# Packing the half-full last chunks of two batches in an MLP, and reordering the first loads

## Chip, cores, metric

One core of a Trainium2 chip. The time is device microseconds for one launch; a run of all kernels here is called fast when it is within 1.5% of the fastest of its kernel, and all runs quoted were. A difference is given as a ratio: the mean time of one kernel's fast runs over the mean of the other's from the same rounds, so not quite the ratio of the medians quoted beside it. Its 95% interval is some 0.1 to 0.15% to each side, about 0.5 us; a difference between two such differences is uncertain by some 0.7 us.

In the profiles PE is TensorE's matrix multiplications and PEld its weight loads, DVE is VectorE, ACT is ScalarE, POOL is GpSimd, SP is SyncE; L356 is line 356 of that kernel. A matmul is written with the shape of its stationary operand (`128*64`: 128 rows, 64 columns; the one that PEld loads) and then that of its moving operand (`128x512`: 512 moving columns). An eviction is the instruction on ACT or DVE that copies a result out of PSUM. A head pair is two heads that are worked on together, and qsrow a table, made from an iota (the numbers 0, 1, 2, ...), by which q is multiplied. `[2.76 <-PE ps_y L356]` says that the engine stood idle for 2.76 us before the line and what ended that.

## The reference, cut to what matters

```python
# batch 8, heads 8, sequence 576, head_dim 64: d_model 512; MLP width 2048
scores = scale * q @ k.T                       # per head
ret    = scores * where(i >= j, gamma**(i-j), 0)
x      = (ret @ v)  -> [batch, 576, 512]
u      = x + (x.T @ U @ V).T                   # low-rank mixer over tokens, rank 32
out    = u + relu(u @ w_ch1) @ w_ch2           # the MLP, 512 -> 2048 -> 512
```

576 tokens are four chunks of 128 and one of 64. That last 64 is what the change is about.

## The kernel before

It is written for a scheduler that fixes each engine's order of instructions and inserts the semaphores; `nc.any` lets it choose ACT or DVE. Per batch: attention (retention in chunks, head pairs one after another through one PSUM buffer `po`), the mixer, the two MLP products.

```python
def make_consts():                       # after batch 0's q, k, v loads are issued
    nc.gpsimd.iota(iota_col, pattern=[[1, SP]], ...)
    ... qsrow = exp(iota_col * log(gamma))       # ACT; q is multiplied by it
    ... U_sb, V_sb loads

def mlp_tail(b, u_t, uT_t):
    y1_t = y1_pool.tile([P, NF, S], BF16, ...)           # y1_pool: bufs=2
    for f in range(NF):                                  # 16
        for half in range(2):                            # 288 tokens each
            for cc in range(NCC):                        # 4
                nc.tensor.matmul(ps_y1[:, 0:HTOK], w1_sb[:, cc, f*P:(f+1)*P],
                                 uT_t[:, cc, t0:t0+HTOK], ...)
            nc.any.tensor_scalar(out=y1_t[:, f, t0:t0+HTOK], in0=ps_y1[:, 0:HTOK],
                                 ..., op0=ALU.max)
    for tcn in range(NC):                                # 5 chunks
        L = P if tcn < NC - 1 else LAST                  # 128 or 64 tokens
        for f in range(NF):
            nc.tensor.matmul(ps_y2[0:L, :], y1_t[:, f, tcn*P:tcn*P+L],
                             w2_sb[:, f, :], ...)
        nc.vector.tensor_tensor(out=o_sb[0:L, :], in0=ps_y2[0:L, :],
                                in1=u_t[0:L, tcn, :], op=ALU.add)
        nc.sync.dma_start(out=out[b, tcn*P:tcn*P+L, :], in_=o_sb[0:L, :])

make_early_consts()
qkv_tiles[0] = qkv_load(0)
make_consts()
qkv_tiles[1] = qkv_load(1)
load_weights()                                           # w1, then w2
# ... attention(0); then per batch: load b+2, mixer(b), attention(b+1), mlp_tail(b)
```

Of the kernel before, what the change touches and what calls it, by code (L numbers as in the profile page):

```python
# [10 lines left out]
BF16 = mybir.dt.bfloat16  # L11
AF = mybir.ActivationFunctionType
ALU = mybir.AluOpType
# [3 lines left out]
def kernel(  # L17
# [11 lines left out]
    nc = tc.nc  # L29

    B, H, S, D = q.shape
    dm = H * D
    dff = moe_w_ch1.shape[1]
    R = moe_U.shape[1]
    P = 128
    NC = (S + P - 1) // P
    LAST = S - (NC - 1) * P
    SP = NC * P
    NHP = H // 2
    NF = dff // P  # L40
    NCC = dm // P
    MAIN = (NC - 1) * P
    HTOK = 288
# [8 lines left out]
    ssb_pool = ctx.enter_context(tc.tile_pool(name="ssb_pool", bufs=8))  # L52
    xu_pool = ctx.enter_context(tc.tile_pool(name="xu_pool", bufs=2))
    mix_pool = ctx.enter_context(tc.tile_pool(name="mix_pool", bufs=2))
    y1_pool = ctx.enter_context(tc.tile_pool(name="y1_pool", bufs=2))
    osb_pool = ctx.enter_context(tc.tile_pool(name="osb_pool", bufs=4))

    ps_sc = ctx.enter_context(tc.tile_pool(name="ps_sc", bufs=2, space=bass.MemoryType.PSUM))
# [10 lines left out]
    iota_col = consts.tile([P, SP], FP32)  # L69
# [7 lines left out]
    def make_early_consts():  # L77
        nc.gpsimd.iota(
            iota_pc, pattern=[[P, NC]], base=0, channel_multiplier=1,
            allow_small_or_imprecise_dtypes=True,  # L80
        )
        nc.gpsimd.memset(lnbias, math.log(scale))
        for h in range(H):
            g = gammas[h]
            nc.scalar.activation(
                out=vscale[:, h, :],
                in_=iota_pc,
                func=AF.Exp,
                bias=lnbias,
                scale=-math.log(g),  # L90
            )

    def make_consts():
        nc.gpsimd.iota(
            iota_col, pattern=[[1, SP]], base=0, channel_multiplier=0,
            allow_small_or_imprecise_dtypes=True,
        )

        for hp in range(NHP):
            for hl in range(2):  # L100
                g = gammas[2 * hp + hl]
                nc.scalar.activation(
                    out=qsrow[hl * 64:(hl + 1) * 64, hp, :],
                    in_=iota_col[hl * 64:(hl + 1) * 64, :],
                    func=AF.Exp,
                    bias=0.0,
                    scale=math.log(g),
                )

        nc.gpsimd.memset(U_sb, 0.0)  # L110
        nc.gpsimd.dma_start(
            out=U_sb[:, 0:NC - 1, 0:R],
            in_=moe_U[0:MAIN, :].rearrange("(c p) r -> p c r", p=P),
        )
        nc.gpsimd.dma_start(out=U_sb[0:LAST, NC - 1, 0:R], in_=moe_U[MAIN:S, :])

        nc.gpsimd.memset(V_sb, 0.0)
        nc.gpsimd.dma_start(out=V_sb[0:R, 0:S], in_=moe_V)
# [1 line left out]
    w1_sb = consts.tile([P, NCC, dff], BF16)  # L120
    w2_sb = consts.tile([P, NF, dm], BF16)

    def load_weights():
        for cc in range(NCC):
            nc.gpsimd.dma_start(
                out=w1_sb[:, cc, :], in_=moe_w_ch1[cc * P:(cc + 1) * P, :]
            )
        for fc in range(NF):
            nc.gpsimd.dma_start(
                out=w2_sb[:, fc, :], in_=moe_w_ch2[fc * P:(fc + 1) * P, :]  # L130
            )

    def qkv_load(b):
        q_all = qkv_pool.tile([P, NC, H, 64], BF16, tag="q_all", name="q_all")
        k_all = qkv_pool.tile([P, NC, H, 64], BF16, tag="k_all", name="k_all")
        v_all = qkv_pool.tile([P, NC, H, 64], BF16, tag="v_all", name="v_all")
        for t_dram, t_sb in ((q, q_all), (k, k_all), (v, v_all)):
            nc.gpsimd.memset(t_sb[LAST:P, NC - 1, :, :], 0.0)  # L138
            for c in range(NC):
                L = P if c < NC - 1 else LAST  # L140
                nc.gpsimd.dma_start(  # L141
                    out=t_sb[0:L, c, :, :],
                    in_=t_dram[b, :, c * P:c * P + L, :].rearrange(
                        "h s d -> s h d"
                    ),
                )
        vs = vscale.rearrange("p h c -> p c h")
        vs_b = vs[:, :, :, None].to_broadcast([P, NC, H, 64])
        for c in range(NC):
            nc.gpsimd.tensor_tensor(  # L150
                out=v_all[:, c, :, :],
                in0=v_all[:, c, :, :],
                in1=vs_b[:, c, :, :],
                op=ALU.mult,
            )
        return q_all, k_all, v_all
# [141 lines left out]
    def mixer_head(b, x_t, u_t, uT_t):  # L298
        ps_at = ps_mix.tile([P, 512], FP32, tag="ps_mix", name="ps_at")
        for c in range(NC):  # L300
            nc.tensor.matmul(  # L301
                ps_at,
                U_sb[:, c, :],
                x_t[:, c, :],
                start=(c == 0), stop=(c == NC - 1),
            )
        at_sb = mix_pool.tile([P, dm], BF16, tag="at_sb", name="at_sb")
        nc.any.tensor_copy(out=at_sb, in_=ps_at)

        for c in range(NC):  # L310
            ps_h = ps_mix.tile([P, 512], FP32, tag="ps_mix", name="ps_h")
            nc.tensor.matmul(  # L312
                ps_h,
                V_sb[:, c * P:(c + 1) * P],
                at_sb,
                start=True, stop=True,
            )
            nc.vector.tensor_tensor(  # L318
                out=u_t[:, c, :], in0=ps_h, in1=x_t[:, c, :], op=ALU.add
            )  # L320

        for c in range(NC):
            ps_ut = ps_sc.tile([P, 4, P], BF16, tag="ps_sc", name="ps_ut")
            for cc in range(NCC):
                nc.tensor.transpose(  # L325
                    ps_ut[:, cc, :],
                    u_t[:, c, cc * P:(cc + 1) * P],
                    ident,
                )
            nc.any.tensor_copy(  # L330
                out=uT_t[:, :, c * P:(c + 1) * P], in_=ps_ut[:, 0:NCC, :]
            )

    def mlp_tail(b, u_t, uT_t):
        y1_t = y1_pool.tile([P, NF, S], BF16, tag="y1_t", name="y1_t")
        for f in range(NF):
            for half in range(2):
                t0 = half * HTOK
                ps_y1 = ps_big.tile([P, 512], FP32, tag="ps_big", name="ps_y1")
                for cc in range(NCC):  # L340
                    nc.tensor.matmul(  # L341
                        ps_y1[:, 0:HTOK],
                        w1_sb[:, cc, f * P:(f + 1) * P],
                        uT_t[:, cc, t0:t0 + HTOK],
                        start=(cc == 0), stop=(cc == NCC - 1),
                    )
                nc.any.tensor_scalar(  # L347
                    out=y1_t[:, f, t0:t0 + HTOK], in0=ps_y1[:, 0:HTOK],
                    scalar1=0.0, scalar2=None, op0=ALU.max,
                )  # L350

        for tcn in range(NC):
            L = P if tcn < NC - 1 else LAST
            ps_y2 = ps_big.tile([P, 512], FP32, tag="ps_big", name="ps_y2")
            for f in range(NF):
                nc.tensor.matmul(  # L356
                    ps_y2[0:L, :],
                    y1_t[:, f, tcn * P:tcn * P + L],
                    w2_sb[:, f, :],
                    start=(f == 0), stop=(f == NF - 1),  # L360
                )
            o_sb = osb_pool.tile([P, dm], FP32, tag="o_sb", name="o_sb")
            nc.vector.tensor_tensor(  # L363
                out=o_sb[0:L, :], in0=ps_y2[0:L, :], in1=u_t[0:L, tcn, :],
                op=ALU.add,
            )
            nc.sync.dma_start(
                out=out[b, tcn * P:tcn * P + L, :], in_=o_sb[0:L, :]
            )

    qkv_tiles = {}
    x_tiles = {}

    make_early_consts()
    qkv_tiles[0] = qkv_load(0)
    make_consts()
    qkv_tiles[1] = qkv_load(1)
    load_weights()

    x_tiles[0] = xu_pool.tile([P, NC, dm], BF16, tag="x_t", name="x_t")  # L380
    attention(0, qkv_tiles[0], x_tiles[0])

    for b in range(B):
        if b + 2 < B:
            qkv_tiles[b + 2] = qkv_load(b + 2)

        u_t = xu_pool.tile([P, NC, dm], BF16, tag="u_t", name="u_t")
        uT_t = xu_pool.tile([P, NCC, SP], BF16, tag="uT_t", name="uT_t")
        with tc.high_priority():
            mixer_head(b, x_tiles[b], u_t, uT_t)  # L390

        if b + 1 < B:
            x_tiles[b + 1] = xu_pool.tile([P, NC, dm], BF16, tag="x_t", name="x_t")
            attention(b + 1, qkv_tiles[b + 1], x_tiles[b + 1])

        mlp_tail(b, u_t, uT_t)


# [28 lines left out]
```

## Time and profile before

| | before |
|---|---|
| time, median of 13 runs | 432.06 us (431.67 to 432.84) |
| span of the profiled run | 430.1 us |
| second-product matmuls (L356) | 640, of which 128 with 64 columns |

The busy row of the page (engine, busy us, share, instructions), and the first product's evictions on ACT (count, busy us, mean ns):

```profile
PE 391.8 (91%) x3248; PEld 232.0 (54%) x3248; DVE 220.9 (51%) x662; ACT 171.7 (40%) x379; POOL 169.1 (39%) x220
...
L347 ACT ACTIVATE y_t<-ps_y 128x288 bf16<-128x288 f32 x226 | 92.9, 411 | 62.9 <-PE ps_y L341 54.3
```

TensorE (PE) is the only engine above 55%. The chain that ended last, in order of time, gives a mark to measure a batch by, the mixer's first product (ps_at), columns start and us:

```profile
136.51 0.86 PE ps_at L301 x4
...
183.91 0.86 PE ps_at L301 x4
...
231.31 0.86 PE ps_at L301 x4
```

Each batch takes 47.40 us. The last chunks, in the timeline (start, us, engine, what; in brackets the idle time before):

```profile
419.16 0.69 DVE L363 TENSOR_TENSOR o_sb<-ps_y,u_t 128x512 f32<-128x512 f32 x1 [2.76 <-PE ps_y L356]
422.50 3.16 PEld L356 LDWEIGHTS <-y_t 128*64 128x64 bf16 x16 [0.42 <-issue]
422.61 0.69 DVE L363 TENSOR_TENSOR o_sb<-ps_y,u_t 128x512 f32<-128x512 f32 x1 [2.76 <-PE ps_y L356]
426.18 0.68 DVE L363 TENSOR_TENSOR o_sb<-ps_y,u_t 64x512 f32<-64x512 f32 x1 [2.88 <-PE ps_y L356]
```

An add follows each chunk's sixteen matmuls, so the distance of the adds is the time of a chunk: 3.45 us for the fourth (419.16 to 422.61), and about that for the chunk of 64, with half the tokens.

### The profile page before, as it was taken

The page shows a single profiled execution, that of the slowest core. Times are in us where ns is not written, and L with a number is a line of the kernel's source. Part 1 is how long each engine was busy: PE and PEld are TensorE (multiplying, and loading weights), DVE is VectorE, ACT ScalarE, POOL GpSimd, SP SyncE. Part 2 cuts the span into 40 slices and gives each one's busy share as a digit, 9 for nine tenths or more (in the row PEclk, how much of TensorE's full clock was granted, in tenths as well). Part 3 has the DMA queues.
Part 4 walks back from the last instruction along what each step waited for, and adds up shares of the span by engine and source line. Part 5 has one row for each costly group of instructions (what it writes and reads, how often), then busy time and mean ns, then how long its engine had stood idle before and what let it go on. Part 6 is the DMA issues. An engine that isn't in the chain of part 4 may idle for free.

```text
span 430.1 us, 8035 instructions
## 1 busy us (share of the span) xinstructions
PE 391.8 (91%) x3248; PEld 232.0 (54%) x3248; DVE 220.9 (51%) x662; ACT 171.7 (40%) x379; POOL 169.1 (39%) x220
## 2 busy tenths in 40 slices
PE   1256489999999999999999999999999999999996
PEld 0034246754675457644665467645765467546742
DVE  0166458751775448652875268643875277541011
ACT  2152136630564226630664136531663046423800
POOL 9999679899986700682048500000000000000000
PEclk9999999999999999999999999999999999999999
DMA  9999999899959910891079810011000100011011
GB/s 73 92 65 109 163 202 154 52 139 112 166 38 86 111 61 2 58 135 73 14 48 80 113 38 2 2 49 62 2 1 26 65 22 2 2 50 61 2 49 62
DMA packets 121334, 28.38 MB, mean 66 GB/s; under 512 B 114097, under 2 KB 116177, under 8 KB 121297
## 3 DMA queue, kind: packets, MB, share of 16 engines
q0 software_dynamic: 116048, 18.43, 58.0%
q1 hardware_dynamic: 5248, 9.44, 6.2%
q8 instruction: 25, 0.41, 0.4%
q14 instruction: 13, 0.10, 0.1%
HBM read 36.85 MB, written 9.44 MB: 108 GB/s over the span
## 4 chain that ended last, share of the span: by engine, by line
PE 88%; POOL 4%; DVE 4%; ACT 3%; issue 1%; DVEq 0%; ACTq 0%; POOLq 0%
PE ps_y L356 33%; PE ps_y L341 30%; PE po L185 3%; PE po L256 3%; PE blk_sc L219 3%; PE ps_h L312 3%; PE ps_at L301 2%; PE psq L164 2%; PE psk L174 2%; PE ps_ut L325 2%; PE po L271 2%; PE blk_sct L238 2%; POOL q_all L141 1%; ACT x_t L264 1%; POOL k_all L141 1%; POOL v_all L150 1%
## 5 line engine op out<-in xcount | busy, mean ns | idle before, releaser
L341 PE MATMUL ps_y<-uT_t,w_sb 128*128 128x288 bf16 x1024 | 155.3, 287 | 0.0
L356 PE MATMUL ps_y<-w_sb,y_t 128*128 128x512 bf16 (+1 forms) x640 | 149.6, 379 | 0.0
L347 ACT ACTIVATE y_t<-ps_y 128x288 bf16<-128x288 f32 x226 | 92.9, 411 | 62.9 <-PE ps_y L341 54.3
L341 PEld LDWEIGHTS <-w_sb 128*128 128x128 bf16 x1024 | 88.5, 98 | 27.8 <-issue 1.4
L356 PEld LDWEIGHTS <-y_t 128*128 128x128 bf16 (+1 forms) x640 | 61.5, 100 | 65.2 <-issue 3.4
L363 DVE TENSOR_TENSOR o_sb<-ps_y,u_t 128x512 f32<-128x512 f32 (+1 forms) x40 | 27.6, 690 | 99.5 <-PE ps_y L356 99.5
L177 ACT COPY kT<-psk 128x640 bf16<-128x640 bf16 x32 | 22.2, 694 | 95.7 <-PE psk L174 95.7
L200 DVE TENSOR_TENSOR S_cur<-po,S_cur 64x64 bf16<-64x64 f32 x192 | 42.3, 220 | 20.0 <-PE po L185 15.5
L227 DVE TENSOR_TENSOR ret_m<-blk_sc,maskbin 128x512 bf16<-128x512 f32 x64 | 42.5, 687 | 12.7 <-PE blk_sc L219 8.3
L150 POOL TENSOR_TENSOR v_all<-v_all,vscale 128x512 bf16<-128x512 bf16 x40 | 41.3, 1052 | 5.6 <-DMA v_all<-in_v_dram 5.0
L318 DVE TENSOR_TENSOR u_t<-ps_h,x_t 128x512 bf16<-128x512 f32 x40 | 27.6, 690 | 27.3 <-PE ps_h L312 27.3
L185 PE MATMUL po<-v_all,k_all 128*128 128x128 bf16 x128 | 29.2, 228 | 9.7 <-POOL v_all L150 4.7
L330 ACT COPY uT_t<-ps_ut 128x512 bf16<-128x512 bf16 x40 | 23.4, 585 | 33.9 <-PE ps_ut L325 33.9
L141 POOL DMA_DIRECT2D q_all<-in_q_dram x40 | 34.2, 879 | 0.0
L141 POOL DMA_DIRECT2D v_all<-in_v_dram x40 | 34.0, 924 | 0.0
L141 POOL DMA_DIRECT2D k_all<-in_k_dram x40 | 33.7, 880 | 0.0
L280 DVE TENSOR_TENSOR x_t<-po,x_t 128x192 bf16<-128x192 f32 x64 | 22.5, 352 | 7.9 <-PE po L271 5.4
L195 DVE CAST S_cur<-po 64x64 bf16<-64x64 f32 x64 | 14.1, 220 | 24.0 <-PE po L185 22.8
L264 ACT CAST x_t<-po 128x512 bf16<-128x512 f32 x31 | 18.1, 585 | 17.7 <-PE po L256 16.9
L164 PE MATMUL psq<-ident,q_all 128*128 128x128 bf16 x160 | 16.3, 230 | 8.8 <-DMA q_all<-in_q_dram 8.7
L138 POOL MEMSET q_all<- 64x512 bf16 x8 | 4.2, 519 | 49.3 <-PE psq L164 49.0
L185 PEld LDWEIGHTS <-k_all 128*128 128x128 bf16 x128 | 12.7, 100 | 18.5 <-issue 4.4
(50 smaller groups left out, 313.6 us busy)
## 6 DMA issues: line engine op xcount, KB each, us to landing
out_dram<-o_sb SPq DMA_DIRECT2D x32, 256.0 KB, 2.0
q_all<-in_q_dram POOLq DMA_DIRECT2D x32, 128.0 KB, 4.4
k_all<-in_k_dram POOLq DMA_DIRECT2D x32, 128.0 KB, 4.4
v_all<-in_v_dram POOLq DMA_DIRECT2D x32, 128.0 KB, 4.5
w_sb<-in_moe_w_ch_dram POOLq DMA_DIRECT2D x4, 512.0 KB, 7.5
w_sb<-in_moe_w_ch_dram POOLq DMA_DIRECT2D x16, 128.0 KB, 5.7
out_dram<-o_sb SPq DMA_DIRECT2D x8, 128.0 KB, 2.2
q_all<-in_q_dram POOLq DMA_DIRECT2D x8, 64.0 KB, 4.7
```

What stands on the lines that cost most here:

```text
L141: nc.gpsimd.dma_start(out=t_sb[0:L, c, :, :], in_=t_dram[b, :, c * P:c * P + L, :].rearrange("h s d -> s h d"),)
L150: nc.gpsimd.tensor_tensor(out=v_all[:, c, :, :], in0=v_all[:, c, :, :], in1=vs_b[:, c, :, :], op=ALU.mult,)
L164: nc.tensor.transpose(psq[:, c, :], q2d, ident)
L185: nc.tensor.matmul(po[:, 5 + (c % 2), :], k2d, v2d, start=True, stop=True,)
L200: nc.vector.tensor_tensor(out=S_cur[pb:pb + 64, :], in0=po[pb:pb + 64, 5 + (c % 2), pb:pb + 64], in1=S_list[c - 1][pb:pb + 64, :], op=ALU.add,
L227: nc.vector.tensor_tensor(out=rt_h[hl][:, :, :], in0=sc_h[hl][:, :, :], in1=maskbin[:, None, :].to_broadcast([P, 4, P]), op=ALU.mult,)
L318: nc.vector.tensor_tensor(out=u_t[:, c, :], in0=ps_h, in1=x_t[:, c, :], op=ALU.add)
L330: nc.any.tensor_copy(out=uT_t[:, :, c * P:(c + 1) * P], in_=ps_ut[:, 0:NCC, :])
L341: nc.tensor.matmul(ps_y1[:, 0:HTOK], w1_sb[:, cc, f * P:(f + 1) * P], uT_t[:, cc, t0:t0 + HTOK], start=(cc == 0), stop=(cc == NCC - 1),)
L347: nc.any.tensor_scalar(out=y1_t[:, f, t0:t0 + HTOK], in0=ps_y1[:, 0:HTOK], scalar1=0.0, scalar2=None, op0=ALU.max,)
L356: nc.tensor.matmul(ps_y2[0:L, :], y1_t[:, f, tcn * P:tcn * P + L], w2_sb[:, f, :], start=(f == 0), stop=(f == NF - 1),)
L363: nc.vector.tensor_tensor(out=o_sb[0:L, :], in0=ps_y2[0:L, :], in1=u_t[0:L, tcn, :], op=ALU.add,)
```

## The change

Intent: put the two halves of 64 tokens of a pair of batches into one chunk of 128, so that a pair needs nine chunks and not ten; and take two waits out of the start by making the iota before the first loads and loading w1 before batch 1's q, k and v. The diff, cut to its core:

```diff
-    y1_pool = ... tile_pool(name="y1_pool", bufs=2)
+    y1_pool = ... tile_pool(name="y1_pool", bufs=1)      # one block per pair of batches
@@ make_early_consts
+        nc.gpsimd.iota(iota_col, ...)                    # was at the head of make_consts
@@ the first product: block columns are [b0 main 512 | b1 main 512 | b0 tail 64 | b1 tail 64]
+        base = (b % 2) * MAIN
+        tail = 2 * MAIN + (b % 2) * LAST
-                nc.any.tensor_scalar(out=y1_t[:, f, t0:t0 + HTOK], in0=ps_y1[:, 0:HTOK], ...)
+                if half == 0:
+                    nc.any.tensor_scalar(out=y1_2b[:, f, base:base + HTOK], ...)
+                else:                                    # 224 columns, then 64
+                    nc.any.tensor_scalar(out=y1_2b[:, f, base + HTOK:base + MAIN], ...)
+                    nc.any.tensor_scalar(out=y1_2b[:, f, tail:tail + LAST], ...)
@@ the second product: chunks 0-3 in the even batch, 4-8 in the odd one
+        if NTC - 1 in chunks:                            # u of b1's tail, moved to partitions 64..127
+          nc.sync.dma_start(out=u_shift[LAST:P, :], in_=u_t1[0:LAST, NC - 1, :])
...
+            else:                                        # the ninth chunk: two adds, two stores
+                nc.vector.tensor_tensor(out=o_sb[0:LAST, :], ..., in1=u_t0[0:LAST, NC - 1, :])
+                nc.vector.tensor_tensor(out=o_sb[LAST:P, :], ..., in1=u_shift[LAST:P, :])
+                nc.sync.dma_start(out=out[b0, MAIN:S, :], in_=o_sb[0:LAST, :])
+                nc.sync.dma_start(out=out[b1, MAIN:S, :], in_=o_sb[LAST:P, :])
@@ the loads
     make_consts()
+    load_w1()
     qkv_tiles[1] = qkv_load(1)
-    load_weights()
+    load_w2()
```

The u tiles get four buffers, as an even batch's u is needed until the odd batch's ninth chunk.

More of the change, by code (lines that the diff above doesn't have):

```diff
@@ L54 @@
     mix_pool = ctx.enter_context(tc.tile_pool(name="mix_pool", bufs=2))
-    y1_pool = ctx.enter_context(tc.tile_pool(name="y1_pool", bufs=2))
+    y1_pool = ctx.enter_context(tc.tile_pool(name="y1_pool", bufs=1))
     osb_pool = ctx.enter_context(tc.tile_pool(name="osb_pool", bufs=4))
@@ L82, in make_early_consts @@
         nc.gpsimd.memset(lnbias, math.log(scale))
+        nc.gpsimd.iota(
+            iota_col, pattern=[[1, SP]], base=0, channel_multiplier=0,
+            allow_small_or_imprecise_dtypes=True,
+        )
         for h in range(H):
@@ L93, in make_consts @@
     def make_consts():
-        nc.gpsimd.iota(
-            iota_col, pattern=[[1, SP]], base=0, channel_multiplier=0,
-            allow_small_or_imprecise_dtypes=True,
-        )
         for hp in range(NHP):
@@ L121, with load_w1 @@
     w2_sb = consts.tile([P, NF, dm], BF16)
-    def load_weights():
+    def load_w1():
         for cc in range(NCC):
@@ L127, in load_weights, with load_w2 @@
             )
+    def load_w2():
         for fc in range(NF):
@@ L332, in mixer_head, with mlp1 @@
             )
-    def mlp_tail(b, u_t, uT_t):
-        y1_t = y1_pool.tile([P, NF, S], BF16, tag="y1_t", name="y1_t")
+    TBLK = 2 * S
+    NTC = TBLK // P
+    def mlp1(b, uT_t, y1_2b):
+        base = (b % 2) * MAIN
+        tail = 2 * MAIN + (b % 2) * LAST
         for f in range(NF):
@@ L346, in mlp_tail, with mlp2 @@
                     )
-                nc.any.tensor_scalar(
-                    out=y1_t[:, f, t0:t0 + HTOK], in0=ps_y1[:, 0:HTOK],
-                    scalar1=0.0, scalar2=None, op0=ALU.max,
-                )
-        for tcn in range(NC):
-            L = P if tcn < NC - 1 else LAST
+                if half == 0:
+                    nc.any.tensor_scalar(
+                        out=y1_2b[:, f, base:base + HTOK], in0=ps_y1[:, 0:HTOK],
+                        scalar1=0.0, scalar2=None, op0=ALU.max,
+                    )
+                else:
+                    nc.any.tensor_scalar(
+                        out=y1_2b[:, f, base + HTOK:base + MAIN],
+                        in0=ps_y1[:, 0:MAIN - HTOK],
+                        scalar1=0.0, scalar2=None, op0=ALU.max,
+                    )
+                    nc.any.tensor_scalar(
+                        out=y1_2b[:, f, tail:tail + LAST],
+                        in0=ps_y1[:, MAIN - HTOK:HTOK],
+                        scalar1=0.0, scalar2=None, op0=ALU.max,
+                    )
+    def mlp2(j, u_t0, u_t1, y1_2b, chunks):
+        b0, b1 = 2 * j, 2 * j + 1
+        if NTC - 1 in chunks:
+          u_shift = osb_pool.tile([P, dm], BF16, tag="u_shift", name="u_shift",
+                                bufs=2)
+          nc.sync.dma_start(out=u_shift[LAST:P, :], in_=u_t1[0:LAST, NC - 1, :])
+        for tcn in chunks:
             ps_y2 = ps_big.tile([P, 512], FP32, tag="ps_big", name="ps_y2")
@@ L356, in mlp_tail @@
                 nc.tensor.matmul(
-                    ps_y2[0:L, :],
-                    y1_t[:, f, tcn * P:tcn * P + L],
+                    ps_y2,
+                    y1_2b[:, f, tcn * P:(tcn + 1) * P],
                     w2_sb[:, f, :],
@@ L362, in mlp_tail @@
             o_sb = osb_pool.tile([P, dm], FP32, tag="o_sb", name="o_sb")
-            nc.vector.tensor_tensor(
-                out=o_sb[0:L, :], in0=ps_y2[0:L, :], in1=u_t[0:L, tcn, :],
-                op=ALU.add,
-            )
-            nc.sync.dma_start(
-                out=out[b, tcn * P:tcn * P + L, :], in_=o_sb[0:L, :]
-            )
+            if tcn < 4:
+                nc.vector.tensor_tensor(
+                    out=o_sb, in0=ps_y2, in1=u_t0[:, tcn, :], op=ALU.add
+                )
+                nc.sync.dma_start(
+                    out=out[b0, tcn * P:(tcn + 1) * P, :], in_=o_sb
+                )
+            elif tcn < 8:
+                c = tcn - 4
+                nc.vector.tensor_tensor(
+                    out=o_sb, in0=ps_y2, in1=u_t1[:, c, :], op=ALU.add
+                )
+                nc.sync.dma_start(
+                    out=out[b1, c * P:(c + 1) * P, :], in_=o_sb
+                )
+            else:
+                nc.vector.tensor_tensor(
+                    out=o_sb[0:LAST, :], in0=ps_y2[0:LAST, :],
+                    in1=u_t0[0:LAST, NC - 1, :], op=ALU.add,
+                )
+                nc.vector.tensor_tensor(
+                    out=o_sb[LAST:P, :], in0=ps_y2[LAST:P, :],
+                    in1=u_shift[LAST:P, :], op=ALU.add,
+                )
+                nc.sync.dma_start(
+                    out=out[b0, MAIN:S, :], in_=o_sb[0:LAST, :]
+                )
+                nc.sync.dma_start(
+                    out=out[b1, MAIN:S, :], in_=o_sb[LAST:P, :]
+                )
     qkv_tiles = {}
     x_tiles = {}
+    u_tiles = {}
+    y1_blocks = {}
     make_early_consts()
@@ L385 @@
             qkv_tiles[b + 2] = qkv_load(b + 2)
-        u_t = xu_pool.tile([P, NC, dm], BF16, tag="u_t", name="u_t")
+        u_tiles[b] = xu_pool.tile([P, NC, dm], BF16, tag="u_t", name="u_t",
+                                  bufs=4)
         uT_t = xu_pool.tile([P, NCC, SP], BF16, tag="uT_t", name="uT_t")
         with tc.high_priority():
-            mixer_head(b, x_tiles[b], u_t, uT_t)
+            mixer_head(b, x_tiles[b], u_tiles[b], uT_t)
         if b + 1 < B:
@@ L394 @@
             attention(b + 1, qkv_tiles[b + 1], x_tiles[b + 1])
-        mlp_tail(b, u_t, uT_t)
+        if b % 2 == 0:
+            y1_blocks[b // 2] = y1_pool.tile(
+                [P, NF, 2 * S], BF16, tag="y1_2b", name="y1_2b"
+            )
+        mlp1(b, uT_t, y1_blocks[b // 2])
+        j = b // 2
+        if b % 2 == 0:
+            mlp2(j, u_tiles[b], None, y1_blocks[j], range(0, 4))
+        else:
+            mlp2(j, u_tiles[b - 1], u_tiles[b], y1_blocks[j], range(4, NTC))
 _INS = ['q', 'k', 'v', 'moe_U', 'moe_V', 'moe_w_ch1', 'moe_w_ch2']
```

## The prediction

> **What bounds the kernel now.** I read the page first (busy shares, slices), then the chain of waits, the groups of TensorE by shape, the waits of the middle, and the timelines of the first 62 us and of the last 50.
>
> ```profile
> PE   1256489999999999999999999999999999999996
> ...
> PE 88%; POOL 4%; DVE 4%; ACT 3%; issue 1%; DVEq 0%; ACTq 0%; POOLq 0%
> ```
>
> The first line is TensorE's busy share in 40 slices of 10.75 us: poor for the first five or six, then 9 to the end. The second is the chain that ended last: 88% of it is TensorE. The stretch table confirms it: from 160 to 400 us every 40 us hold 39.96 to 40.00 us of TensorE work, and asked for TensorE's waits between 90 and 400 us the trace names none. So there are two stages with different limits: a start of about 60 us in which TensorE waits for others, and a long body in which each matmul that goes is time gained.
>
> ```profile
> L341 PE MATMUL ps_y<-uT_t,w_sb 128*128 128x288 bf16 x1024 | 155.3, 287 | 0.0
> L356 PE MATMUL ps_y<-w_sb,y_t 128*128 128x512 bf16 x512 | 121.0, 379 | 0.0
> L356 PE MATMUL ps_y<-w_sb,y_t 128*64 128x512 bf16 x128 | 29.1, 380 | 0.0
> ```
>
> Groups of TensorE by shape (rows*columns of the stationary operand, then the moving operand). A batch has 576 tokens, four chunks of 128 and one of 64. The second MLP product (L356) uses tokens as the stationary operand: a chunk of 64 loads half the columns and still lasts 380 ns a matmul against 379, because the 512 moving columns set the time. Half of that work is empty array.
>
> ```profile
> 392.97 15.79 PE ps_y L341 x128
> 408.76 17.40 PE ps_y L356 x80
> ```
>
> The chain's last pieces, batch 7 with nothing beside it: 17.40/80 = 217 ns from one L356 matmul to the next, 15.79/128 = 123 ns for L341. The means of 379 and 287 include the overlapping pipe; costs are worked with 217 and 123.
>
> The start:
>
> ```profile
> 14.75 0.69 ACT L177 COPY kT<-psk 128x640 bf16<-128x640 bf16 x1 [11.10 <-PE psk L174]
> 20.81 5.98 ACT L102 ACTIVATE qsrow<-iota_col 64x640 bf16<-64x640 f32 x8 [5.36 <-POOL iota_col L94]
> ...
> 22.32 0.49 DVE L167 TENSOR_TENSOR qT<-psq,qsrow 128x640 bf16<-128x640 bf16 x1 [1.33 <-ACT qsrow L102]
> ...
> 22.96 0.61 PE L219 MATMUL blk_sc<-qT,kT 64*128 64x128 bf16 x8 [2.48 <-DVE qT L167]
> ```
>
> Timelines of ACT, DVE and TensorE. The first head pair's k is transposed and copied at 15.4 us, but its q must be scaled by a table (qsrow) made from an iota that GpSimd only does at 20.1 us, behind four scalings of v. So the scores start at 22.96.
>
> ```profile
> 29.32 0.29 PE L185 MATMUL po<-v_all,k_all 128*128 128x128 bf16 x1 [0.73 <-DVE x_t L286]
> ...
> 44.54 0.29 PE L185 MATMUL po<-v_all,k_all 128*128 128x128 bf16 x1 [0.94 <-DVE x_t L286]
> ...
> 51.06 1.87 PE L301 MATMUL ps_at<-x_t,U_sb 128*128 128x512 bf16 x4 [0.92 <-DVE x_t L280]
> ...
> 60.14 1.16 PE L341 MATMUL ps_y<-uT_t,w_sb 128*128 128x288 bf16 x4
> ```
>
> The po buffer exists once, so each head pair's first k-v product waits for the adds of the pair before: the four pairs run one after another (29.32, 37.32, 44.54 us for the second to fourth), the mixer follows at 51.06 and the MLP at 60.14. This start is latency, not DMA: no wait there is for w1.
>
> **What the Trainium skill says.** "TensorE: Matmul & The Clock Gate", section "Back-to-back issue gap", gives N/2.4 + 2.5 ns for an isolated warm stream, 215.8 at N = 512 and 122.5 at N = 288. The trace agrees: 217 and 123. The same section's 131 ns for a sustained N = 512 stream is not seen here. The section "Step-by-step: what each phase is for" says that the time is the number of moving columns; the 380 against 379 above agrees, and it is why packing two half-full stationary operands into one pays fully. "ScalarE: Activation LUTs", section "What ACT_TABLE_LOAD costs", gives 186 ns + 0.833 ns per element for an ACTIVATE with immediate operands, and an overlap of about 93 ns back to back. The trace: copies of 128 and 512 columns last 268 and 585 ns (0.826 ns per column on 162), and a copy of 0.69 us at 204.07 is followed by the next at 204.66, an overlap of 0.1 us. I use the trace's figures.
>
> **The change part by part.**
>
> 1. Packing. Two batches share one block of 1,152 tokens: eight chunks of 128, and the two halves of 64 as a ninth. L356 goes from 8 batches x 5 chunks x 16 = 640 matmuls to 4 x 9 x 16 = 576. The order of the built kernel shows where: even batches now end with four chunks, odd ones keep five. 64 matmuls x 217 ns = 13.9 us, all in stretches in which TensorE was 100% busy. **-13.9 us.**
>
> 2. Evictions. The second half of each first-product row must be split: 224 columns to the main part, 64 to the tail, 128 instructions more. By the fit above, 224 columns cost 162 + 185 = 347 ns and 64 cost 215, against 411 for 288: about 150 ns more, 16 times a batch, 2.4 us a batch. The order puts nearly all on ACT (468 instructions, before 336). In a first-product stretch (203.5 to 230.1 us) ACT was busy 16.7 of 26.6 us; with this about 19, or 72%. In the last batch, where nothing else pads TensorE, a row pair costs ACT 411 + 347 + 215 - 3 x 100 of overlap = some 0.7 us, and TensorE 8 x 123 = 0.99 us. So ACT keeps up; the three PSUM banks should absorb bursts mostly. I allow **+0.7 us**.
>
> 3. The iota goes ahead of the q loads. It costs 0.66 us of GpSimd before the first load, so v is scaled some 1.6 us later than 20.9 at worst (about 22.4, with a memset that the order puts ahead of the fifth scaling). But the table is done near 10 us, scores of pairs 0 and 1 are made while v is awaited, and pair 0's output products need only v: about 22.5 us, before 24.6 to 26.2. Adding the copy (0.6 to 0.9), the state product (0.4) and the four adds (1.1) the second pair starts near 25.7 instead of 29.32. After it the serial chain is as before, 7 to 7.7 us a pair and 6.5 for the last, so the mixer comes at 46 to 48 us, before 51.06. Gain 3 to 5 us, I take **-3.5 us**.
>
> 4. w1 is loaded ahead of batch 1's q, k and v. w1 is 4 x 512 KB at the 200 GB/s that the stretches from 48 to 64 us show: 10.5 us, landing near 37. Batch 1's 1.77 MB at the 125 to 135 GB/s of 28 to 40 us follow until 49 to 51. Its first v is wanted at about 49, right after the mixer's first product. That just fits; in part 3 I took the low side for it. Without this part the MLP, now wanted at 56 us, would meet w1's old landing near 55. So it guards part 3 and gains nothing itself.
>
> 5. The y block is single, the u buffers are four. The next pair's first eviction must wait for the ninth chunk, but TensorE runs that chunk first anyway. 0 us. The u_shift copy (64 x 512 bf16) has over 10 us until it is needed.
>
> 6. The end. The last chunk now needs two adds of 64 partitions; one of 64 lasts 683 ns. The second store starts that much later: **+0.7 us.**
>
> Sum: -13.9 + 0.7 - 3.5 + 0.7 = -16.0 us; 431.93 - 16.0 = 415.9, called **416.0 us**, 3.7% faster.
>
> **The rivals.**
>
> *ACT takes over.* ACT has 19 us more work (128 x 150 ns) and also carries the copies that attention waits for (kT, 74.5 us of idle before it in the body, so mostly not pressed). If one in five of these microseconds reached TensorE, it would cost 4 us: 419 to 420. For it: in bursts such as 214.4 to 217 us ACT is 80% busy. Against it: no TensorE wait at all in the body today.
>
> *The start does not gain, as batch 1's data come late.* DMA runs one queue; if w1 takes longer or the POOL queue stalls on outstanding transfers, v of batch 1 lands at 53 or later and the mixer, which is interleaved with its products in TensorE's fixed order, waits. Then parts 3 and 4 give 0: 419.5. If they even lose 3 us, 422.5.
>
> *The packing gains less than its matmuls*, if the saved time in even batches uncovers a wait of the next attention for its data or for the mixer. For it: the even body shrinks by 3.5 us. Against it: q, k, v of later batches are loaded tens of us ahead (POOL idles from 240 us on). It would make some 420.
>
> *The start gains more.* Pipelined score work might shorten every pair to 6.5 us: 413 to 414.
>
> **Range and chances.** The packing is almost arithmetic (13.5 to 14.3). The start is the open term, -5 to +1, then ACT, 0 to +3. From -18.5 to -11: 413.4 to 421. I take 412.5 to 420.5. Faster by over 2% means below 423.3; only the loss of the start's gain, with ACT exposed too, misses it: 95% faster, 4.5% same, 0.5% slower.
>
> **What would show it.** Right: 576 second-product matmuls, all 128*128, 217 ns apart at the end; periods of 47.4 us for odd batches and 43.9 for even ones; the scores at 16 to 17 us, the mixer at 46 to 48 and the MLP at 55 to 57; no TensorE waits for ACT in the body. Wrong: idle before L346 released by ACT; batch 1's k-v product waiting on POOL's scaling of v for over 2 us; periods that don't shrink by 3.5 us; a last store more than 1 us later after the last matmul than now.

## The result, and the profile after

415.02 us median of 8 runs (414.42 to 415.24), before 432.06; ratio 0.9602, interval 0.9593 to 0.9612. That is 17.2 us less; 16.0 had been predicted.

The page after, in the same order as before: busy row, TensorE's slices, chain, then the groups that answer to L341 and L356 and to the evictions.

```profile
PE 378.1 (91%) x3184; PEld 226.0 (55%) x3184; DVE 217.1 (53%) x657; ACT 190.8 (46%) x512; POOL 169.1 (41%) x220
...
PE   1465589999999999999999999999999999999995
...
PE 83%; POOL 7%; DMA 4%; ACT 2%; DVE 1%; issue 1%; DVEq 0%; POOLq 0%
...
L379 PE MATMUL ps_y<-w_sb,y_2b 128*128 128x512 bf16 x576 | 134.7, 379 | 0.0
...
L353 ACT ACTIVATE y_2b<-ps_y 128x288 bf16<-128x288 f32 x118 | 48.3, 410 | 21.9 <-PE ps_y L346 19.7
...
L358 ACT ACTIVATE y_2b<-ps_y 128x224 bf16<-128x224 f32 x117 | 42.0, 359 | 21.9 <-PE ps_y L346 17.8
...
L363 ACT ACTIVATE y_2b<-ps_y 128x64 bf16<-128x64 f32 x125 | 28.0, 224 | 4.8 <-DVE y_2b L358 1.0
```

TensorE is as full as before with 64 matmuls fewer; ACT has 19.1 us more. In the chain DMA and POOL have gained a share (4% and 7%): they are the start, in which loads now come closer to being used. The chain's marks:

```profile
177.14 0.86 PE ps_at L302 x4
...
220.64 0.86 PE ps_at L302 x4
...
268.44 0.86 PE ps_at L302 x4
```

43.50 and 47.80 us, 91.30 for a pair against 2 x 47.40 = 94.80. That is 3.50 us a pair, 14.0 for the four. The timeline of TensorE at the start:

```profile
16.06 0.61 PE L220 MATMUL blk_sc<-qT,kT 64*128 64x128 bf16 x8 [0.78 <-ACT kT L178]
...
25.49 0.29 PE L186 MATMUL po<-v_all,k_all 128*128 128x128 bf16 x1 [0.29 <-DVE x_t L287]
...
45.83 1.87 PE L302 MATMUL ps_at<-x_t,U_sb 128*128 128x512 bf16 x4 [0.92 <-DVE x_t L281]
48.55 0.27 PE L186 MATMUL po<-v_all,k_all 128*128 128x128 bf16 x1 [0.85 <-DMA v_all<-in_v_dram]
...
56.03 1.16 PE L346 MATMUL ps_y<-uT_t,w_sb 128*128 128x288 bf16 x4
```

The scores start 6.9 us earlier (22.96 before), the second head pair 3.8, the mixer 5.2, the first MLP product 4.1. The 1.1 us between the last two numbers is lost from the fourth line on: batch 1's k-v products, which TensorE's order has amid the mixer, wait for v, now queued behind w1 (0.85 us there, 0.75 us at the next one, 49.57 us). The end:

```profile
408.39 0.68 DVE L402 TENSOR_TENSOR o_sb<-ps_y,u_t 64x512 f32<-64x512 f32 x1 [2.76 <-PE ps_y L379]
...
409.11 0.69 DVE L406 TENSOR_TENSOR o_sb<-ps_y,u_shift 64x512 f32<-64x512 f32 x1
409.83 0.47 SPq L413 DMA_DIRECT2D out_dram<-o_sb  x1
```

The second add follows the first, and its store is issued 0.73 us after the other's.

### The profile page after: what moved, and what is told of

It reads as the page before. It is cut to its first block, busy times and chain, and to the rows that moved or that the text cites.

```text
span 413.2 us, 8035 instructions
## 1 busy us (share of the span) xinstructions
PE 378.1 (91%) x3184; PEld 226.0 (55%) x3184; DVE 217.1 (53%) x657; ACT 190.8 (46%) x512; POOL 169.1 (41%) x220
## 4 chain that ended last, share of the span: by engine, by line
PE 83%; POOL 7%; DMA 4%; ACT 2%; DVE 1%; issue 1%; DVEq 0%; POOLq 0%
PE ps_y L346 31%; PE ps_y L379 30%; PE po L186 3%; PE ps_h L313 3%; DMA w_sb<-in_moe_w_ch_dram 3%; PE po L257 3%; PE ps_ut L326 2%; PE blk_sc L220 2%; PE psk L175 2%; PE ps_at L302 2%; PE blk_sct L239 2%; PE psq L165 2%; PE po L272 2%; POOL v_all L142 2%; POOL k_all L142 2%; DMA v_all<-in_v_dram 1%
## 5 line engine op out<-in xcount | busy, mean ns | idle before, releaser
L379 PE MATMUL ps_y<-w_sb,y_2b 128*128 128x512 bf16 x576 | 134.7, 379 | 0.0
L379 PEld LDWEIGHTS <-y_2b 128*128 128x128 bf16 x576 | 54.3, 98 | 57.4
L353 ACT ACTIVATE y_2b<-ps_y 128x288 bf16<-128x288 f32 x118 | 48.3, 410 | 21.9 <-PE ps_y L346 19.7
L201 DVE TENSOR_TENSOR S_cur<-po,S_cur 64x64 bf16<-64x64 f32 x192 | 42.3, 220 | 21.5 <-PE po L186 17.4
L358 ACT ACTIVATE y_2b<-ps_y 128x224 bf16<-128x224 f32 x117 | 42.0, 359 | 21.9 <-PE ps_y L346 17.8
L228 DVE TENSOR_TENSOR ret_m<-blk_sc,maskbin 128x512 bf16<-128x512 f32 x64 | 42.4, 687 | 16.9 <-PE blk_sc L220 11.3
L395 DVE TENSOR_TENSOR o_sb<-ps_y,u_t 128x512 f32<-128x512 f32 x16 | 11.1, 692 | 48.0 <-PE ps_y L379 48.0
L363 ACT ACTIVATE y_2b<-ps_y 128x64 bf16<-128x64 f32 x125 | 28.0, 224 | 4.8 <-DVE y_2b L358 1.0
L387 DVE TENSOR_TENSOR o_sb<-ps_y,u_t 128x512 f32<-128x512 f32 x16 | 11.0, 689 | 27.9 <-PE ps_y L379 27.9
```

Of the source, the lines that this page charges most:

```text
L201: nc.vector.tensor_tensor(out=S_cur[pb:pb + 64, :], in0=po[pb:pb + 64, 5 + (c % 2), pb:pb + 64], in1=S_list[c - 1][pb:pb + 64, :], op=ALU.add,
L228: nc.vector.tensor_tensor(out=rt_h[hl][:, :, :], in0=sc_h[hl][:, :, :], in1=maskbin[:, None, :].to_broadcast([P, 4, P]), op=ALU.mult,)
L353: nc.any.tensor_scalar(out=y1_2b[:, f, base:base + HTOK], in0=ps_y1[:, 0:HTOK], scalar1=0.0, scalar2=None, op0=ALU.max,)
L358: nc.any.tensor_scalar(out=y1_2b[:, f, base + HTOK:base + MAIN], in0=ps_y1[:, 0:MAIN - HTOK], scalar1=0.0, scalar2=None, op0=ALU.max,)
L363: nc.any.tensor_scalar(out=y1_2b[:, f, tail:tail + LAST], in0=ps_y1[:, MAIN - HTOK:HTOK], scalar1=0.0, scalar2=None, op0=ALU.max,)
L379: nc.tensor.matmul(ps_y2, y1_2b[:, f, tcn * P:(tcn + 1) * P], w2_sb[:, f, :], start=(f == 0), stop=(f == NF - 1),)
```

## The experiments

My theory: the packing's gain is its matmuls; the start's gain is the iota's and adds to it; the evictions lie beside TensorE; the last add costs 0.7 us. The rivals: evictions reach TensorE, w1's move is what frees the start (or only costs), the packing uncovers a wait. All outputs are right. The last column is (ratio - 1) x 432.

| run | what | median us | ratio | us against before |
|---|---|---|---|---|
| changed kernel | all | 415.02 | 0.9602 | -17.2 |
| p_only | packing | 418.61 | 0.9682 | -13.7 |
| iw_only | iota, w1 | 428.22 | 0.9904 | -4.1 |
| i_only, i_again | iota | 429.75, 428.93 | 0.9936, 0.9930 | -2.8, -3.0 |
| w_only | w1 | 432.02 | 0.9995 | -0.2 |
| pi_only, pi_again | packing, iota | 414.76, 414.98 | 0.9600, 0.9612 | -17.3, -16.8 |
| evict_one | all, no split evictions | 415.24 | 0.9609 | -16.9 |
| evict_more | all, 128 more evictions | 415.79 | 0.9625 | -16.2 |
| tail_last | all, ninth chunk first in last pair | 413.74 | 0.9574 | -18.4 |
| tail_first | all, ninth chunk first in all pairs | 412.24 | 0.9549 | -19.5 |
| kvwq | tail_first, batch 1 loaded k, v, w1, q | 411.80 | 0.9532 | -20.2 |

### The parts, one by one

**p_only**: the kernel before with the packing, the iota and w1 left where they were.

> The kernel before with the packing alone (shared block of 1,152 tokens, nine chunks a pair, split evictions, two adds at the end); iota and w1 stay where they were. My theory (the gains of the body and of the start are independent): 64 matmuls x 217 ns = -13.9 us, +0.7 for the last add, 0 to +0.7 for evictions: 12.5 to 13.2 us under before, 418.9 to 419.6. First first-product matmul of batch 0 still at 60 us. Rival (evictions cost): only 9 to 10 us, with TensorE waits for ACT. Rival (the packing is worth more as later data come in better): over 14 us.

13.7 us (13.5 by the medians). The first product of batch 0 is at 60.16 us in its trace, as before. More than the 12.5 to 13.2 expected, so nothing of the size of the rival (a loss of 3 to 4 us to evictions) is there; TensorE's waits between 90 and 390 us come to 1.7 us in all. What evictions do cost is tested below.

**iw_only**: the other half of the change alone.

```diff
@@ make_early_consts
+        nc.gpsimd.iota(iota_col, ...)
@@ make_consts
-        nc.gpsimd.iota(iota_col, ...)
@@
     make_consts()
+    load_w1()
     qkv_tiles[1] = qkv_load(1)
-    load_weights()
+    load_w2()
```

> The kernel before with the early iota and w1 ahead of batch 1's loads, no packing. My theory: the start's gain alone, 3.5 to 4.1 us (the trace of the changed kernel has the first first-product matmul 4.1 us earlier), so 428 us. Rival (the gain of the start is given back in batch 0's attention, whose data come later): 0 to 2 us.

4.1 us. With the packing's 13.7 this makes 17.8; both together gave 17.2, so the parts add up within the intervals.

**i_only** and **w_only**: the two parts of that, each alone.

> The kernel before with the early iota alone. My theory as predicted (w1 guards the gain): the mixer comes about 5 us earlier, at 46 us, but the first first-product matmul then meets w1, which lands near 56 us: a gain of 3 to 4 us, about as with both moves. Rival A (moving w1 is needed): w1 holds the first product up, gain under 2 us. Rival B (moving w1 only costs, by delaying batch 1's v by 1.1 us at the mixer): gain of 5 us, more than with both.

> The kernel before with w1 ahead of batch 1's loads alone. My theory: no gain, as nothing waited for w1: 0, or a loss up to 1 us if batch 1's v comes after 52.7 us, when the trace of before used it. Rival (w1's late landing bounded the start): gain of 2 us or more.

w1's move alone does nothing (-0.2). The iota alone gives 2.8, between my theory and rival A. Its timeline shows why:

```profile
55.32 0.92 PE L340 MATMUL ps_y<-uT_t,w_sb 128*128 128x288 bf16 x3
57.48 0.42 PE L340 MATMUL ps_y<-uT_t,w_sb 128*128 128x288 bf16 x1 [1.24 <-DMA w_sb<-in_moe_w_ch_dram]
```

The first product is reached at 55.32 us, 4.8 earlier than before, and its fourth matmul waits 1.24 us for the last part of w1. So both waits exist: without the move for w1, with it for v of batch 1. The move exchanges one for the other. (How v came to be late: with w1 ahead, GpSimd's issuing of batch 1's k loads stood 2.50 and 1.48 us in the changed kernel until parts of w1 had landed.)

**pi_only**: the changed kernel with w1 put back.

```diff
-    load_w1()
     qkv_tiles[1] = qkv_load(1)
+    load_w1()
```

> The changed kernel with w1 put back behind batch 1's loads (packing and early iota stay). If moving w1 neither gains nor costs: within 0.7 us of the changed kernel, 415.0. If it guards the start: 2 us or more slower than the changed kernel. If it only costs by delaying batch 1's v: 1 us faster, 414.

17.3 us against 17.2: with the packing in, w1's move neither gains nor costs. By the medians the iota thus seemed to give 3.9 us on top of the packing but 2.3 alone.

> The early iota alone once more, beside the next run on one chip. Before it gained 2.3 us alone, and 3.9 us on top of the packing, on two different jobs. If w1's landing only jitters between chips: both gains alike here, within 0.7 us. If packing changes the wait for w1: again 1.5 us apart.

> Packing and early iota once more, beside the run above: 17.2 us under before if as last time; some 15.6 us if the early iota gains only 2.3 here too (packing alone gave 13.5).

-3.0 and -16.8: on top of the packing's 13.7 the iota gave 3.1 here and 3.6 in the first pair, alone 3.0 and 2.8. These agree within the intervals; the 1.5 us were scatter. The wait for w1 in the profiled runs is 1.2 and 1.3 us in the two of the iota alone, and only a weight load held 0.5 and 0.6 us in the two with the packing, which leaves perhaps 0.6 us of difference that I did not settle.

The traces show another thing that can make such differences. For a while after the first product TensorE's matmuls run at half speed (see kvwq), and the moment at which that ends moves from run to run. i_only and i_again are the same kernel: in the one, seven first-product matmuls from 61.60 us took 1.82 us, in the other seven from 61.03 took 1.03. At the mixer of batch 2 the two are 1.4 us apart (134.94 and 133.56 us), and iw_only, at 133.40, hardly differs from the second. So the 1.1 to 1.3 us by which iw_only beats the two runs of the iota alone are not shown to be w1's.

### The evictions

**evict_one**: the odd batch's tokens are laid tail first, so that the two tails meet in the middle and every eviction is one of 288 columns again.

```diff
-        base = (b % 2) * MAIN
-        tail = 2 * MAIN + (b % 2) * LAST
+        base = (b % 2) * S                   # block: [b0 main | b0 tail | b1 tail | b1 main]
@@ evictions
-                if half == 0: ...            # three forms
+                nc.any.tensor_scalar(out=y1_2b[:, f, base + t0:base + t0 + HTOK], ...)
@@ mixer: uT of an odd batch holds its tail in columns 0..63
+            o0, L = (c * P, P) if even else (LAST + c * P, P) if c < NC - 1 else (0, LAST)
```

> The changed kernel with the odd batch's tokens laid tail first, so that the two halves meet in the middle of the block (chunk 4) and every eviction of the first product is one instruction of 288 columns again; 128 instructions fewer, some 19 us of ACT work less. My theory (ACT's extra work lies beside TensorE): same within 0.7 us. Rival (evictions reach TensorE): 2 to 4 us faster.

**evict_more**: the first half is split as well.

```diff
-                    nc.any.tensor_scalar(out=y1_2b[:, f, base:base + HTOK], in0=ps_y1[:, 0:HTOK], ...)
+                    for e0, e1 in ((0, 224), (224, HTOK)):
+                        nc.any.tensor_scalar(out=y1_2b[:, f, base + e0:base + e1], in0=ps_y1[:, e0:e1], ...)
```

> The changed kernel with the first half's eviction split as well (224 and 64 columns), 128 instructions more, so the suspected cost is doubled; about 1.15 us of ACT work for each 0.99 us of TensorE in the last batch, less the overlap of 0.1 us each. My theory: at most 1 us slower, as ACT still keeps up. Rival (evictions reach TensorE): 2 us or more slower, with TensorE waits for ACT.

Taking the 128 instructions away gave nothing (-16.9 against -17.2); adding 128 more cost some 1.0 us. So the split evictions of the change cost nothing that these intervals could show (-0.3 +/- 0.8 us, thus at most 0.5 for 19 us of ACT work), and as many again begin to show (1.0 +/- 0.7). All three kernels have the same three TensorE waits of 0.2 us that the trace puts down to an eviction, one at each boundary between pairs; they are looked at next. In the last batch's first product (the stretch from 375 to 391.5 us), ACT is busy 14.15 of 16.50 us with evict_more, and TensorE 16.50: still not the bound.

### The end, and the boundary between pairs

**tail_first**: the ninth chunk is the first of the odd batch's five.

```diff
-            mlp2(j, u_tiles[b - 1], u_tiles[b], y1_blocks[j], range(4, NTC))
+            mlp2(j, u_tiles[b - 1], u_tiles[b], y1_blocks[j],
+                 [NTC - 1] + list(range(4, NTC - 1)))
```

> The changed kernel with the odd batches' ninth chunk (the two halves) taken first and not last, so that the kernel ends with one add and one store. My theory (the second add of 64 partitions stands on the path that ends last): 0.7 us faster than the changed kernel. Rival (its store was hidden, or the copy of u that the chunk needs now comes late): 0 or slower.

2.3 us by the ratios to the kernel before (0.9549 and 0.9602), 2.8 by the medians, not 0.7: a miss, and the most useful of the runs. Where the rest comes from is on DVE at the boundary from batch 3 to batch 4. The changed kernel (timeline of DVE):

```profile
240.02 0.68 DVE L402 TENSOR_TENSOR o_sb<-ps_y,u_t 64x512 f32<-64x512 f32 x1 [2.76 <-PE ps_y L379]
240.73 0.70 DVE L406 TENSOR_TENSOR o_sb<-ps_y,u_shift 64x512 f32<-64x512 f32 x1
241.46 0.49 DVE L168 TENSOR_TENSOR qT<-psq,qsrow 128x640 bf16<-128x640 bf16 x1
```

With the ninth chunk first:

```profile
239.01 0.69 DVE L395 TENSOR_TENSOR o_sb<-ps_y,u_t 128x512 f32<-128x512 f32 x1 [2.76 <-PE ps_y L379]
239.62 0.48 DVE L168 TENSOR_TENSOR qT<-psq,qsrow 128x640 bf16<-128x640 bf16 x1
```

The next attention needs qT, and two adds stand before it instead of one. In the changed kernel qT begins 1.64 us after TensorE's first transposes of that attention (239.82), in the other 0.81 (238.81). TensorE's fixed order fills the time with ten first-product matmuls rather than six and then still stops:

```profile
242.10 0.33 PE L220 MATMUL blk_sc<-qT,kT 64*128 64x128 bf16 x5 [0.19 <-ACT y_2b L358]
```

The line names an ACT eviction, which ended at 241.97 us; qT ended at 241.95, and the scores read qT and not the eviction. With single evictions (evict_one) the same stop of 0.19 us stands there, so it is not the split. The second add is late for TensorE in another way too: it still reads one of the three PSUM buffers of the MLP, and the weight loads of two of the ten matmuls stood 0.21 us for it. Both go when the ninth chunk comes first; which of them costs how much was not separated. With the ninth chunk first, the chain's marks are:

```profile
175.91 0.86 PE ps_at L302 x4
...
219.62 0.86 PE ps_at L302 x4
...
266.79 0.86 PE ps_at L302 x4
```

A pair loses 0.42 us at its boundary in the changed kernel (91.30 us there, 90.88 here). From the mixer of batch 2 to that of batch 7, which holds three such boundaries, the changed kernel takes 230.40 us (129.34 to 359.74) and this one 228.96 (128.72 to 357.68). The fixed order did not hide the second add: an engine that isn't the bound was late for the one that is.

That leaves a finding on the kernel before. A pair takes 94.80 us there and 90.88 with the ninth chunk first: 3.92, more than sixteen matmuls at 217 ns (3.47). The chunk of 64 took 3.57 us against 3.45, and TensorE's weight loads stood 0.42 us on going into the 64-column chunk and 0.41 on leaving it, here for batch 7's first product:

```profile
392.90 15.55 PEld L341 LDWEIGHTS <-w_sb 128*128 128x128 bf16 x128 [0.41 <-issue]
```

The 0.12 us more of that chunk are measured. By batches the marks give 43.71 and 47.17 us with the ninth chunk first, 0.22 and 0.23 us under what the matmuls alone would make of 47.40 (43.93 and 47.40). So a chunk of 64 seems to cost 0.22 us more than one of 128; that the 0.10 beyond the 0.12 are lost on leaving it is inferred from the equal gap and was not tried alone. In the changed kernel the boundary hid this part of the gain.

**tail_last**: the same in the last pair alone, to tell the end from the boundaries.

```diff
+                 ([NTC - 1] + list(range(4, NTC - 1))) if b == B - 1 else range(4, NTC))
```

> The changed kernel with the ninth chunk taken first in the last pair alone. The run with all pairs so was 2.8 us faster than the changed kernel, of which the traces put 0.7 on the end, some 0.4 on each of three boundaries between pairs (the next pair's first products wait there for the second add, which holds one of three PSUM banks) and 0.6 on a moment at half clock near 58 us. If that reading holds: 0.7 us faster than the changed kernel, 414.3 on its scale. If the gain is all of the end: 2 us or more.

1.2 us, interval about 0.7 to each side: the end's share, somewhat more than the 0.73 of the trace but within its reach, and 1.1 short of all pairs. The stretch from batch 2's to batch 7's mixer is 230.33 us in it (129.30 to 359.63), as in the changed kernel; so the boundaries are where the rest is. I had put another 0.6 us on TensorE's clock near 58 us: in the trace of tail_first five transposes there take 0.44 us, in the changed kernel's 0.74. One profile each; left as scatter of the start.

### The start, once more

**kvwq**: tail_first, with batch 1's loads in the order of use.

```diff
+        if w1_between:                       # batch 1
+            load(k, k_all); load(v, v_all)
+            load_w1()
+            scale_v()
+            load(q, q_all)
```

> Tail chunk first in all pairs, and batch 1's loads in the order in which they are used: k, v, then w1, then q. In the changed kernel's trace the mixer waits about 1.1 us for batch 1's v behind w1; with w1 behind all three the first product waits for w1. My theory: both waits go, 1.1 us under the run with the tail first, 411. Rival (the start is bounded elsewhere): same as that run, 412.2.

411.80 us, ratio 0.9532 (0.9519 to 0.9545) against tail_first's 0.9549 (0.9536 to 0.9563): 0.7 us less with intervals that overlap, so not settled. Both waits are gone in its trace: the first product is at 55.17 us, 0.9 earlier. But the gain ends in the next lines:

```profile
57.92 1.65 PE L362 MATMUL ps_y<-uT_t,w_sb 128*128 128x288 bf16 x6
```

and in tail_first:

```profile
58.46 0.90 PE L346 MATMUL ps_y<-uT_t,w_sb 128*128 128x288 bf16 x6
```

From the start of one matmul to the next these are about 240 ns in the first line and 123 in the second (a line's time ends when its last matmul does, and one of them alone is recorded with 0.28 to 0.45 us, so it is not six times the distance): half speed, until 59.5 us in one trace and until 57 in the other. Both then reach the last batch's first product at 373.6 us. The profiled run of kvwq was the slowest of its four (412.29 us, the others 411.44, 411.07 and 412.16), so this tells why that run gained nothing, and not what the four gained together. What the start saves can be lost to when TensorE gets its full rate. The page's clock row shows 9 there; it does not show this.

## Why the prediction was right

**Time.** 416.0 predicted, 412.5 to 420.5, 95% for faster; 415.02 measured.

**Packing, -13.9.** The pairs' marks give -14.0, p_only as a whole -13.7. The step "the 512 moving columns set the time" held: 576 matmuls, all 128 columns wide, still 379 ns. That the size agreed so closely was luck, two errors that cancel, neither of which the prediction had: doing without 64-column chunks gains 0.45 us a pair more, and the two adds at a pair's boundary take 0.42 back (tail_first). They show where the prediction's own sign failed: it had 47.4 us for odd batches and 43.9 for even ones, and 47.80 and 43.50 came. It counted the second add at the end alone; that was wrong.

**Evictions, +0.7.** ACT got 19.1 us more, as worked out (19); 359 and 224 ns for the two pieces, 347 and 215 had been taken. The cost to TensorE was none that could be measured (evict_one, at most 0.5 us). The term was mis-sized: 0.7 for about 0.

**Iota, -3.5.** The predicted steps came in order and nearly on time: scores at 16.06 us ("16 to 17"), second pair 25.49 (25.7), mixer 45.83 (46 to 48), first product 56.03 (55 to 57). The second and third pairs took 6.9 us each where 7 to 7.7 had been taken. The first product came 4.1 us earlier, and iw_only gained 4.1, but both hold w1's move too; the iota alone gave 2.8 and 3.0 us, and with the packing 3.1 and 3.6. So the 3.5 was near. One reading of the trace was too wide: "This start is latency, not DMA" holds for the chain of head pairs, but in the first 15 us TensorE waited 8.7 us for q's loads and 3.2 for k's.

**w1, "guards part 3 and gains nothing itself".** Half right. Alone it gives nothing (w_only), with the iota without packing perhaps 1.1 to 1.3 us (iw_only against i_again and i_only, not shown to be w1's), and with the packing nothing (pi_only). It does hold off a wait of 1.2 us, but puts a wait of 1.1 us for batch 1's v in its place; "that just fits" was wrong by that much. The rival that the queue "stalls on outstanding transfers" thus came true in part: it stalled for 4.0 us, but v was in use at 48.55 us and not only at 53.

**End, +0.7.** 0.73 us in the trace, 1.2 +/- 0.7 by the clock (tail_last).

**Single y block, 0.** No wait on it is seen in the trace; a run with two blocks does not fit into the memory (its build stops: 72 kb per partition wanted, 68.125 left), and was not made.

**Sum.** -14.0 - 4.1 + 0.7 (the second add) + 0 = -17.4, measured -17.2. The prediction was short by 1.2 us, which is the evictions' 0.7 and the start's 0.6 to within the scatter. The range's upper end of -11 is not the sum of its terms at their worst (-13.5 + 1 + 3 + 0.7 = -8.8), but takes it that they don't all fall together.

## What to carry to other kernels

Where moving columns set a matmul's time, count stationary operands that are not full: two halves joined are a whole matmul saved, and the work of splitting and joining, 19 us on an engine with slack, cost no more than 0.5 us here. But look at what stands in a slack engine's queue just before something the bound engine waits for: here a second add of 0.7 us, ahead of the next attention's first multiplication, cost TensorE 0.4 us at each boundary between pairs, and moving the joined chunk from last to first gave 2.3 us in all. Moving one load ahead of others that are wanted at the same moment can exchange one wait for another: here w1's for v's, 1.2 us for 1.1.

## What the Trainium skill lacked or had wrong

- "TensorE: Matmul & The Clock Gate", "Back-to-back issue gap": the sustained 131 ns for a 512-column matmul with its weight load is not seen. Eighty such pairs took 17.28 us in the changed kernel, 216 ns each; its isolated figure, 215.8, fits.
- The same page, "LDWEIGHTS (loading the stationary operand)", gives columns / 1.2 ns, 107 for 128 columns; the trace has 98 (95 to 99). For 64 columns the formula makes 53 ns, and the trace of the kernel before has 110.
- No page has a cost for going between 128 and 64 stationary columns: weight loads stood 0.42 us on going in and 0.41 on leaving, and the chunk of 64 took 3.57 us against 3.45.
- The same page, "Part 1: The HAM clock gate (the "warmup" mystery)", has half rate until sustained work; the traces agree (240 against 123 ns for 288 columns). But full rate came at 57 us in tail_first and at 59.5 in kvwq, with the first product at nearly the same time (56.05 and 55.17), and in two profiles of one kernel by 61.0 us (i_again) and only at about 63 (i_only). That is more than the +/- 0.5 us that the page names in one place, and fits better what it says in another of the same section, that the window is free-running and the number of slow matmuls varies from run to run.
